# Moving masking from VectorE to ScalarE, with P*V a slot later, in a fused attention and FFN kernel

## The chip, the cores and the metric

One core of a Trainium2 chip runs the kernel. The metric is device time in microseconds (us) for one execution, lower is better. The profile and the trace are those of one execution. A run counts as "slow" when it took over 1.5% longer than the fastest run of the same kernel, else as "fast".

## The reference

Attention with a threshold, then a multiplicative FFN without a nonlinearity. There are 8 batches, 8 heads, 576 positions and 64 dimensions per head.

```python
scores = scale * np.matmul(q, k.transpose(0, 1, 3, 2))
thresh = np.max(scores, axis=-1, keepdims=True) - tau
scores = np.where(scores >= thresh, scores, -1000000000.0)
attn = np.exp(scores - max); attn = attn / (sum(attn) + 1e-09)    # shortened
x = attn @ v, heads side by side                                   # (4608, 512)
a = x @ w1; b = x @ w2
out = (a * b @ w3) @ w_out
```

## The kernel before

The kernel is a hand-made pipeline of slots. Heads go in 32 pairs, and a pair has nine chunks of 128 query rows by 576 keys: four for each head, and one *mixed* chunk that holds the last 64 rows of both heads. There are 288 chunks. P*V is the product of probabilities and values. PSUM is the memory that the kernel's matmuls write to; a piece of it can be used again once another engine has read it out. Slot `t` starts the scores of chunk `t` on TensorE, the maximum of chunk `t-1` on VectorE, and the masking of chunk `t-4`. Masking has two paths:

- Path P: ScalarE takes the exponential (0.67 us) one slot ahead, VectorE masks with one *select* (0.87 us).
- Path A: ScalarE does all of it in two passes, `mask_a` (0.77 us) in the chunk's slot and `mask_b` (0.67 us) one slot later.

The finished probabilities are transposed by DMA (for the first pairs by TensorE), and P*V of a whole pair starts a fixed number of slots after its last chunk. FFN matmuls fill TensorE's time in between.

```python
LAG = 4
EARLY = 4                      # pairs whose probabilities TensorE transposes
PATH = "AAP"                   # chunk c takes PATH[c % 3]; a mixed chunk is c = 9 n + 8
...
def mask_b(c):
    nc.scalar.activation(place(*stream[c]), chunks.pop(c)["y"][:, :], AF.Exp, scale=-CUT)
    leave_probs(*stream[c])                    # starts the transpose
...
def select(c):
    t = chunks.pop(c)
    nc.vector.scalar_tensor_tensor(out=place(*stream[c]), in0=t["sc"][:, :], scalar=t["thr"],
                                   in1=t["e"][:, :], op0=ALU.is_ge, op1=ALU.mult)
    leave_probs(*stream[c])
...
for units, follow in groups:                   # when P*V of a pair runs
    c = max(where[n, 8 if i == 4 else 2 * i + hh] for n, hh, i in units)
    c = max(c + LAG + 3, last + 2)
    at(c, attended, att, 0.9)                  # P*V, first half
    at(c + 1, attended, att, 0.9)              # P*V, second half
    norms[c + 2] = att                         # normalise on VectorE
    at(c + 3, attended, att, 0.35)             # transpose the result
...
for t in range(end + 1):                       # one slot
    scores(t)
    maximum(t - 1)
    if t in norms:
        next(norms[t])
    leave()                                    # what is left of the FFN steps
    while late:
        late.pop(0)()                          # PSUM copies of transposes
    ...
    c = t - LAG
    if PATH[c % 3] == "A":
        mask_a(c)
        waiting.append(c)
    while waiting and waiting[0] < c:
        mask_b(waiting.pop(0))
    if PATH[(c + 1) % 3] == "P":
        exponent(c + 1)
    if PATH[c % 3] == "P":
        select(c)
    ...
```

(The tests that a chunk number is in range are cut.)

With `9 n + 8` modulo 3 always 2, **every mixed chunk of the kernel before (the last batch aside) takes path P**. No line of the code says so; it follows from the period of three.

The softmax here doesn't subtract the row's maximum and nothing guards it: scores larger than these inputs give would overflow.

## Time and profile before

| | before |
|---|---|
| time, median of 4 runs | 565.11 us (563.97 to 567.57) |
| TensorE / VectorE / ScalarE busy | 488 / 453 / 389 us of 564.0 |
| 37th maximum pass starts at | 84.6 us |
| 253rd maximum pass starts at | 456.6 us |
| last maximum pass starts at | 514.8 us |

The maximum passes, one per chunk, are a good clock for the pipeline: the 37th ends the start-up, from the 37th to the 253rd the kernel is in its steady middle, after the last one only FFN work is left. Their times are read from the trace.

First, the page of the kernel before: busy time with its share of the span and the number of instructions, then the shares of the chain of waits.

```profile
PE 488.2 (87%) x4964; PEld 334.6 (59%) x4964; DVE 452.7 (80%) x1046; ACT 389.3 (69%) x678; POOL 182.2 (32%) x256
...
PE 43%; DVE 30%; DMA 10%; issue 7%; ACT 7%; POOL 2%; SPq 1%; DVEq 0%; ACTq 0%; POOLq 0%
```

The chain passes through both TensorE (PE) and VectorE (DVE). The table of windows tells where: from 100 to 450 us both are near 90% busy, and from 30 to 60 us VectorE is at 94%. Columns are the stretch, its length, busy us of each engine with the number of instructions, the granted TensorE clock, the DMA share and GB/s.

```profile
30.00:60.00 30.00, 22.40 (x262) 17.39 (x261) 28.32 (x58) 16.36 (x27) 23.73 (x35) 0.89 0.97 202
60.00:100.00 40.00, 33.40 (x409) 25.06 (x407) 32.72 (x76) 23.43 (x40) 10.60 (x12) 0.96 0.23 49
100.00:450.00 350.00, 319.21 (x3308) 218.60 (x3306) 312.53 (x723) 270.18 (x470) 127.05 (x161) 0.99 0.91 188
```

What TensorE waited for from 100 to 450 us (total us, times, longest):

```profile
PE S L244 <- DVE sc L269: 11.6, 12, 1.7
PE av L356 <- DMA pT<-pm: 6.6, 5, 2.7
PE S L250 <- DVE sc L269: 3.4, 5, 1.6
```

`S` are scores, waiting for the maximum pass to free their PSUM; `av` is P*V, waiting for transposed probabilities. The last FFN parts, in the timeline of TensorE (start, length, instruction):

```profile
547.25 0.60 PE L428 MATMUL ab<-xm,w1b 128*128 128x256 bf16 x4
548.00 0.60 PE L428 MATMUL ab<-xm,w2b 128*128 128x256 bf16 x4
548.43 0.60 PE L428 MATMUL ab<-xm,w1b 128*128 128x256 bf16 x4
```

From one step to the next (two groups of four) 1.18 us pass. A group that follows at once starts 0.43 us after the one before, so the work is 0.87 us, and 0.31 us of a step is lost. It is read as a wait for one of two PSUM banks; the list of waits does not name it, and part 5 of the change tests it.

Finally two groups of VectorE, with mean ns of one:

```profile
L335 DVE SCALAR_TENSOR_TENSOR pm<-sc,thr,e 128x576 bf16<-128x576 f32 x66 | 57.2, 866 | 11.4 <-ACT e L331 11.2
L277 DVE TENSOR_SCALAR thr<-mx 128x3 f32<-128x3 f32 x96 | 34.2, 356 | 0.0
```

The first waits 11 us for the exponential. The second, the subtraction that makes the threshold, has a median of 162 ns but a mean of 356: 28 of its 96 instances take 0.44 to 1.13 us (0.80 in the mean), and all 28 overlap a GpSimd operation.

### The profile page before, as it was taken

To read this page: it belongs to the slowest core of one execution; us is meant where nothing else is said; L and a number is where in the kernel's file an instruction comes from. 1 tells how busy PE (TensorE), PEld (TensorE's weight loads), DVE (VectorE), ACT (ScalarE), POOL (GpSimd) and SP (SyncE) were. 2 spreads that over 40 slices of the span, in tenths; PEclk is the share of its full clock that TensorE was granted. 3 is DMA by queue.
4 is the path that set the end of the run, shared out by engine and by line. 5 is a ranking of instruction groups with operands and counts; after the bars stand their busy time and mean duration, and the time that the engine had idled before them with its cause. 6 is when DMAs were issued, how large, how long until landed. Compare 5 with 4: busy or idle time off the path is not lost.

```text
span 564.0 us, 13012 instructions
## 1 busy us (share of the span) xinstructions
PE 488.2 (87%) x4964; PEld 334.6 (59%) x4964; DVE 452.7 (80%) x1046; ACT 389.3 (69%) x678; POOL 182.2 (32%) x256
## 2 busy tenths in 40 slices
PE   1777987988999889899899889999988899798985
PEld 0555665655666566565666567666656666465663
DVE  1899878989997998689899979899879977695321
ACT  2455555777887778668788778878867778588332
POOL 3986423063402632172305440353165300000000
PEclk9988989999999999999999999999989999799999
DMA  7997520987889697989999796989999667456310
GB/s 157 278 237 154 110 59 23 199 177 168 154 180 239 134 208 168 256 124 179 220 193 188 157 238 149 215 143 221 223 197 242 119 141 157 78 85 160 52 65 39
DMA packets 203374, 91.43 MB, mean 162 GB/s; under 512 B 169008, under 2 KB 194608, under 8 KB 203312
## 3 DMA queue, kind: packets, MB, share of 16 engines
q1 hardware_dynamic: 199920, 85.36, 71.1%
q0 software_dynamic: 3392, 5.24, 5.5%
q8 instruction: 39, 0.64, 0.5%
q14 instruction: 23, 0.19, 0.1%
HBM read 39.32 MB, written 9.44 MB: 86 GB/s over the span
## 4 chain that ended last, share of the span: by engine, by line
PE 43%; DVE 30%; DMA 10%; issue 7%; ACT 7%; POOL 2%; SPq 1%; DVEq 0%; ACTq 0%; POOLq 0%
PE ab L428 11%; DVE sc L269 11%; PE yp L443 10%; PE S L244 9%; PE av L356 4%; DVE ab L420 4%; DMA pT<-pm 4%; DVE pm L335 3%; DVE thr L277 3%; DMA pTm<-pms_74 3%; ACT y L321 2%; DVE pms_75 L335 2%; PE tp L205 2%; PE wp L132 2%; PE S L250 2%
## 5 line engine op out<-in xcount | busy, mean ns | idle before, releaser
L269 DVE TENSOR_SCALAR_CACHE_REDUCE sc<-S 128x576 f32<-128x576 f32 x288 | 213.4, 749 | 19.8 <-PE S L244 16.9
L321 ACT ACTIVATE y<-sc,thr 128x576 bf16<-128x576 f32 x192 | 140.6, 768 | 62.7 <-DVE thr L277 62.4
L244 PE MATMUL S<-kT,qT 128*128 128x288 bf16 x464 | 127.5, 294 | 15.1 <-DVE sc L269 11.8
L325 ACT ACTIVATE pm<-y 128x576 bf16<-128x576 bf16 x190 | 127.6, 672 | 1.5 <-DMA pT<-pm 1.4
L244 PE MATMUL S<-kB,qT 128*128 128x288 bf16 x464 | 127.3, 294 | 0.5 <-DMA kB<-kT 0.5
L244 PEld LDWEIGHTS <-qT 128*128 128x128 bf16 x928 | 89.0, 100 | 64.9 <-issue 17.0
L420 DVE TENSOR_TENSOR ab<-ah,ab 128x512 bf16<-128x512 bf16 (+1 forms) x88 | 51.7, 587 | 36.8 <-PE ab L428 32.2
L417 ACT ACTIVATE ah<-ab 128x512 bf16<-128x512 f32 (+1 forms) x88 | 45.2, 514 | 41.0 <-PE ab L428 39.4
L428 PE MATMUL ab<-xm,w2b 128*128 128x512 bf16 (+1 forms) x288 | 68.8, 362 | 4.1 <-DVE ab L420 0.9
L443 PE MATMUL yp<-wcb,ab 128*128 128x512 bf16 x288 | 71.2, 379 | 1.3 <-DVE ab L420 1.2
L428 PE MATMUL ab<-xm,w1b 128*128 128x512 bf16 (+1 forms) x288 | 68.0, 359 | 2.2 <-DVE ab L420 2.2
L335 DVE SCALAR_TENSOR_TENSOR pm<-sc,thr,e 128x576 bf16<-128x576 f32 x66 | 57.2, 866 | 11.4 <-ACT e L331 11.2
L331 ACT ACTIVATE e<-sc 128x576 f32<-128x576 f32 x96 | 64.3, 670 | 0.0
L356 PEld LDWEIGHTS <-pT 128*128 128x128 bf16 x1320 | 51.2, 98 | 11.8 <-DMA pT<-pm 7.6
L428 PEld LDWEIGHTS <-w2b 128*128 128x128 bf16 x352 | 33.3, 98 | 28.3 <-issue 10.2
L428 PEld LDWEIGHTS <-w1b 128*128 128x128 bf16 x352 | 33.0, 98 | 24.9 <-issue 6.3
L165 POOL CAST khl<-kf 128x512 bf16<-128x512 f32 x31 | 19.9, 641 | 72.9 <-PE tp L205 41.8
L166 POOL TENSOR_TENSOR qhl<-qf,qhl 128x512 bf16<-128x512 f32 x32 | 39.0, 1220 | 10.8 <-ACT qhl L568 8.3
L443 PEld LDWEIGHTS <-ab 128*128 128x128 bf16 x288 | 26.8, 98 | 24.8 <-issue 1.7
L166 POOL TENSOR_TENSOR khl<-kf,khl 128x512 bf16<-128x512 f32 x31 | 39.0, 1258 | 2.5
L435 ACT ACTIVATE ys<-yp 128x512 f32<-128x512 f32 x36 | 21.4, 595 | 25.0 <-PE yp L443 24.4
L165 POOL CAST khlt<-kt 128x256 bf16<-128x256 f32 x7 | 3.6, 511 | 95.5 <-DMA kt<-in_k_dram 95.5
(124 smaller groups left out, 778.6 us busy)
## 6 DMA issues: line engine op xcount, KB each, us to landing
kB<-kT SPq DMA_DIRECT2D x58, 144.0 KB, 4.0
out_dram<-ys SPq DMA_DIRECT2D x16, 512.0 KB, 3.6
kf<-in_k_dram SPq DMA_DIRECT2D x15, 512.0 KB, 4.5
qf<-in_q_dram SPq DMA_DIRECT2D x15, 512.0 KB, 5.6
vf<-in_v_dram SPq DMA_DIRECT2D x15, 512.0 KB, 4.8
pT<-pm SPq DMA_TRANSPOSE x112, 3.8
kt<-in_k_dram SPq DMA_DIRECT2D x16, 64.0 KB, 5.1
w1b<-in_moe_w_dram POOLq DMA_DIRECT2D x4, 256.0 KB, 6.0
```

Source lines behind the costliest of these rows:

```text
L166: lo.tensor_tensor(hl[1], src, hl[0], ALU.subtract)
L244: nc.tensor.matmul(sp[:, half, 0:HB], lhsT=t["qT"][:, q0:q0 + 128], rhs=kk[w][:, c0:c0 + HB], start=(w == 0), stop=(w == 1))
L269: nc.vector.tensor_scalar(sc[:, :].rearrange("p (a b) -> p a b", a=2), sp[:, :, 0:HB], 1.0, -3e38, ALU.mult, ALU.max, accum_out=maxima[c / ...
L321: nc.scalar.activation(t["y"][:, :], t.pop("sc")[:, :], AF.Prelu, scale=-1.0, bias=t.pop("thr"), alpha=0.125 / CUT)
L325: nc.scalar.activation(place(*stream[c]), chunks.pop(c)["y"][:, :], AF.Exp, scale=-CUT)
L331: nc.scalar.activation(t["e"][:, :], t["sc"][:, :], AF.Exp, scale=0.125)
L335: nc.vector.scalar_tensor_tensor(out=place(*stream[c]), in0=t["sc"][:, :], scalar=t["thr"], in1=t["e"][:, :], op0=ALU.is_ge, op1=ALU.mult)
L356: nc.tensor.matmul(dst, lhsT=lhsT, rhs=rhs, start=(g == 0), stop=(g == 4))
L417: return lambda: nc.scalar.activation(ah[:, 0:nt], p[:, 0:nt], AF.Copy)
L420: return lambda: nc.vector.tensor_tensor(ab[:, 0:nt], ah[:, 0:nt], p[:, 0:nt], ALU.mult)
L428: nc.tensor.matmul(p[:, 0:nt], lhsT=w[:, c, f * 128:(f + 1) * 128], rhs=x(c), start=(c == 0), stop=(c == 3))
L443: nc.tensor.matmul(yp[0:c1 - c0, :], lhsT=abs_[f][:, c0:c1], rhs=wcb[:, f, :], start=(f == 0), stop=(f == NF - 1))
```

## The change

Its intent is to take work off VectorE, and to give transposes and the last FFN parts more room.

1. `PATH` becomes `"AAAP"`: VectorE masks 72 chunks in place of 96. The exponential comes two slots ahead, with a third buffer.
2. The op on row sums of mixed chunks goes; 1e30 in the sums' column makes the reciprocal of the unwanted sums vanish.
3. P*V starts one slot later (not in the last batch); normalisation stands behind the select; the result's transpose comes a slot later; four buffers in place of two for mixed chunks.
4. Early transposes cover three pairs in place of four, and ScalarE makes part of the PSUM copies.
5. After the last slot, FFN steps use the three larger PSUM buffers of the scores.

```diff
-    EARLY = 4
+    EARLY = 3
+    LATER = 4
...
+            nc.gpsimd.memset(t[96:97, :, 0, D:D + 1], 1e30)
+            nc.gpsimd.memset(t[64:65, :, 1, D:D + 1], 1e30)
...
-    PATH = "AAP"
+    PATH = "AAAP"
...
+            if i % 2:
+                late.append(lambda: nc.scalar.activation(to, fro, AF.Copy))
+            else:
+                late.append(lambda: nc.vector.tensor_copy(to, fro))
...
-        if len(mixed) == 2:
-            nc.vector.tensor_tensor(rcp[:, 1, nu - 2:nu], rcp[:, 1, nu - 2:nu], diag[:, :], ALU.mult)
...
+                if w is w1b and wide():
+                    both = psum.tile([128, 2, 512], FP32, tag="S", name="both", bufs=3)
+                    p = both[:, 0, :]
...
-        c = max(c + LAG + 3, last + 2)
+        c = max(c + LAG + (LATER if units[0][0] < NPAIR - NP else 3), last + 2)
...
-        at(c + 3, attended, att, 0.35)
+        at(c + 4, attended, att, 0.35)
...
-            if t in norms:
-                next(norms[t])
             leave()
...
-            if 0 <= c + 1 < total and PATH[(c + 1) % 3] == "P":
-                exponent(c + 1)
-            if 0 <= c < total and PATH[c % 3] == "P":
+            if 0 <= c + 2 < total and PATH[(c + 2) % 4] == "P":
+                exponent(c + 2)
+            if 0 <= c < total and PATH[c % 4] == "P":
                 select(c)
+            if t in norms:
+                next(norms[t])
```

(Cut: the test for path "A", buffer counts, among them eight in place of ten for transposed probabilities, the removed constants, the FFN's start a slot later, the slot counter that `wide()` reads.)

More of the change, by code (lines that the diff above doesn't have):

```diff
@@ L59 @@
     ident2 = constp.tile([128, 64], BF16, tag="ident2", name="ident2")
-    diag = constp.tile([128, 2], FP32, tag="diag", name="diag")
     w1b = constp.tile([128, 4, d_ff], BF16, tag="w1b", name="w1b")
@@ L64 @@
     xt = constp.tile([128, NP, B, R], BF16, tag="xt", name="xt")
-    pms = [constp.tile([128, 640], BF16, tag=f"pms{i}", name=f"pms{i}") for i in range(2)]
+    pms = [constp.tile([128, 640], BF16, tag=f"pms{i}", name=f"pms{i}") for i in range(4)]
     vbs = [constp.tile([128, 2, 4, VW], BF16, tag=f"vb{i}", name=f"vb{i}") for i in range(5)]
@@ L72, in constants @@
     def constants():
-        nc.gpsimd.memset(diag[:, :], 0.0)
-        for hh in range(2):
-            nc.gpsimd.memset(diag[64 * hh:64 * hh + 64, hh:hh + 1], 1.0)
         nc.vector.tensor_tensor(ident2[:, :], ident[:, 0:64], ident[:, 64:128], ALU.add)
@@ L87, in constants @@
             nc.gpsimd.memset(t[:, S:640], 0.0)
+            nc.gpsimd.memset(t[0:64, S:S + 1], 1.0)
+            nc.gpsimd.memset(t[64:128, S + 32:S + 33], 1.0)
     wl = {}
@@ L284, in place @@
             pairs[n]["pm"] = work.tile([128, 2, S], BF16, tag="pm", name="pm", bufs=3)
-        return pairs[n]["pm"][:, hh, :] if hh < 2 else pms[n % 2][:, 0:S]
+        return pairs[n]["pm"][:, hh, :] if hh < 2 else pms[n % 4][:, 0:S]
     turning = []
@@ L291, in turn_probs @@
         nb = 9 if i < 4 else 5
-        pT = work.tile([128, nb, 128], BF16, tag="pT" if i < 4 else "pTm", name="pT", bufs=10 if i < 4 else 5)
+        pT = work.tile([128, nb, 128], BF16, tag="pT" if i < 4 else "pTm", name="pT", bufs=8 if i < 4 else 5)
         pairs[n]["pT", i] = pT
@@ L299, in go @@
             clock["pe"] += 0.07 * nb
-            late.append(lambda: nc.vector.tensor_copy(pT[:, :, :].rearrange("p g f -> p (g f)"), tp[:, 0:nb * 128]))
+            to, fro = pT[:, :, :].rearrange("p g f -> p (g f)"), tp[:, 0:nb * 128]
+            if i % 2:
+                late.append(lambda: nc.scalar.activation(to, fro, AF.Copy))
+            else:
+                late.append(lambda: nc.vector.tensor_copy(to, fro))
         turning.append(go)
@@ L309, in leave_probs @@
         elif hh == 1:
-            t["pT", i] = work.tile([128, 9, 128], BF16, tag="pT", name="pT", bufs=10)
+            t["pT", i] = work.tile([128, 9, 128], BF16, tag="pT", name="pT", bufs=8)
             nc.sync.dma_start_transpose(t["pT", i][:, :, :], t["pm"][:, :, :].rearrange("p a b -> p (a b)"))
         elif hh == 2 and n < EARLY:
-            turn_probs(n, 4, pms[n % 2][:, :])
+            turn_probs(n, 4, pms[n % 4][:, :])
         elif hh == 2:
             t["pT", 4] = work.tile([128, 5, 128], BF16, tag="pTm", name="pTm", bufs=5)
-            nc.sync.dma_start_transpose(t["pT", 4][:, :, :], pms[n % 2][:, :])
+            nc.sync.dma_start_transpose(t["pT", 4][:, :, :], pms[n % 4][:, :])
     def mask_a(c):
@@ L329, in exponent @@
         t = chunks[c]
-        t["e"] = work.tile([128, S], FP32, tag="e", name="e", bufs=2)
+        t["e"] = work.tile([128, S], FP32, tag="e", name="e", bufs=3)
         nc.scalar.activation(t["e"][:, :], t["sc"][:, :], AF.Exp, scale=0.125)
@@ L345, in attend @@
         nu = len(units) // 2
-        mixed = [j for j, (n, hh, i) in enumerate(units) if i == 4]
         for un, (n, hh, i) in enumerate(units):
@@ L360, in attend @@
         nc.vector.reciprocal(rcp[:, :, 0:nu], a5[:, :, :, D])
-        if len(mixed) == 2:
-            nc.vector.tensor_tensor(rcp[:, 1, nu - 2:nu], rcp[:, 1, nu - 2:nu], diag[:, :], ALU.mult)
-        elif mixed:
-            r = rcp[:, :, 0:nu].rearrange("p a (u h) -> p a u h", h=2)
-            nc.vector.tensor_tensor(r, r, diag[:, :].unsqueeze(1).unsqueeze(1).to_broadcast([128, 2, nu // 2, 2]),
-                                    ALU.mult)
         x = work.tile([128, 10, D], BF16, tag="x", name="x", bufs=2)
@@ L409, in leave, with wide @@
             pending.append(way)
+    def wide():
+        return clock["slot"] >= end
     def ffn(x, nt, store):
@@ L423, in ffn @@
             ah = work.tile([128, 512], BF16, tag="ah", name="ah", bufs=2)
-            ab = work.tile([128, 512], BF16, tag="ab", name="ab", bufs=12)
+            ab = work.tile([128, 512], BF16, tag="ab", name="ab", bufs=9)
+            both = None
             for w in (w1b, w2b):
-                p = psum.tile([128, 512], FP32, tag="m", name="ab")
+                if w is w1b and wide():
+                    both = psum.tile([128, 2, 512], FP32, tag="S", name="both", bufs=3)
+                    p = both[:, 0, :]
+                elif both:
+                    p = both[:, 1, :]
+                else:
+                    p = psum.tile([128, 512], FP32, tag="m", name="ab")
                 for c in range(4):
@@ L470 @@
     background = []
-    clock = {"pe": 0.0}
+    clock = {"pe": 0.0, "slot": 0}
     def step():
@@ L551 @@
         norms[c + 2] = att
-        at(c + 3, attended, att, 0.35)
+        at(c + 4, attended, att, 0.35)
         if follow:
-            at(c + 4, lambda follow: push(*[f(*a) for f, *a in follow]), follow)
-    end = last + 5
+            at(c + 5, lambda follow: push(*[f(*a) for f, *a in follow]), follow)
+    end = last + 6
     with tc.manual_schedule():
@@ L583 @@
         for t in range(end + 1):
+            clock["slot"] = t
             if t < total:
@@ L596 @@
             c = t - LAG
-            if 0 <= c < total and PATH[c % 3] == "A":
+            if 0 <= c < total and PATH[c % 4] == "A":
                 mask_a(c)
@@ L616 @@
                     step()
+        clock["slot"] = end
         while step():
```

## The prediction

> **What bounds the kernel now.** No engine is saturated over the span. TensorE is busy 488 of 564.0 us, VectorE 453, ScalarE 389 (the page's first part). From 100 to 450 us (table of windows) TensorE is busy 91%, VectorE 89%, ScalarE 77%: TensorE and VectorE hold each other up in turn. The chain of waits agrees: TensorE 43%, VectorE 30%, DMA 10%. TensorE is visibly idle 31 us in that middle: 12 us before scores, mostly on VectorE's maximum pass that frees their PSUM, 8 us before P*V, mostly on DMA transposes. From 30 to 100 us it is idle 14 us, 11 before the early probability transposes, again on VectorE. From 533 us on, each FFN step takes 1.18 us although its eight matmuls need 0.87 us: two PSUM banks do not let TensorE run ahead.
>
> **What changes, in durations of this trace.**
> - Masking by VectorE falls from 96 to 72 chunks: 24 x 0.80 us (866 ns less overlap) = 19 us off VectorE; ScalarE gets 24 x 0.77 = 18 us more.
> - The op on row sums goes: 29 x 0.19 = 5.6 us off VectorE.
> - Early transposes: 20 PSUM copies (14 us) on VectorE become 9 (6 us). Six move to ScalarE, an estimated 1.1 us each from its 0.59 us for 512 columns and 0.38 us for 256. The fourth pair's five go to DMA, little used then (23% from 60 to 100 us); TensorE loses 3 us.
> - Sum: VectorE -33 us, ScalarE +25 us (some 82% in the middle), TensorE -3 us.
> - P*V a slot later, four buffers for mixed chunks and an earlier exponential remove waits: 7 us of TensorE on transposes, 3 us of VectorE on one, part of 14 us in which VectorE waits for the exponential.
> - Last FFN parts: 16 steps lose 0.31 us each, 5 us, all critical.
> - Against it: normalisation now stands behind the select, so P*V's PSUM comes free about 1 us later, once per pair; DMA, 0.86 to 0.98 busy through most of the middle, gets more transposes and less time.
>
> Not touched: 28 of the 96 threshold subtractions take about 0.8 us instead of 0.16, and all 28 overlap a GpSimd operation. The Trainium skill, "SBUF — State Buffer", says that VectorE and GpSimd share a port pair held as an exclusive lock; these durations agree.
>
> **How much is critical.** Early stage: 5 us. Middle: VectorE loses about 18 us; I count half, 9 us, plus 3 us of removed DMA and exponential waits, less 2 us for the later norm: 10 us. Tail: 5 us. Sum 20 us: 544 us. TensorE then runs at about 94% in the middle.
>
> **Predicted: 544 us, 534 to 556 with 8 in 10. Faster by over 2%: 0.77; within 2%: 0.21; slower: 0.02.**
>
> **What would show the steps.** 72 selects, VectorE busy near 420, ScalarE near 413. Middle: TensorE's waits for the maximum pass fall from 12 to about 6 us, those for transposes to near 0. Early: the 11 us of idle before probability transposes fall under 5. Tail: FFN steps 0.87 us apart.
>
> **What would make it wrong.** ScalarE works in order and now carries two passes for three chunks running; if masks come late, transposes and P*V shift and VectorE's freed time turns into waits on ScalarE. DMA near saturation could make transposes later than the extra slot hides. The later norm could hold scores' PSUM. Then 555 or more. Or the coupling was tighter than half: 535.

## The result and the profile after

| | before | after |
|---|---|---|
| time, median of 4 runs each | 565.11 us | 546.32 us (545.83 to 547.55) |
| ratio | | 0.9665 (95% interval 0.9625 to 0.9706) |
| TensorE / VectorE / ScalarE busy | 488 / 453 / 389 us | 476 / 416 / 408 us |
| up to the 37th maximum pass | 84.6 us | 79.7 us |
| 37th to 253rd | 372.0 us | 365.0 us |
| 253rd to the last | 58.2 us | 54.1 us |
| after the last | 49.2 us | 45.7 us |

A ratio is the mean time of one kernel's fast runs over that of the other's in the same rounds, so it is not quite the quotient of the medians. Where two experiments are compared below, the quotient of their ratios to the kernel before is used, since not all ran on the same chip.

The total lies 2 us from the forecast. The page after:

```profile
PE 475.8 (87%) x4862; PEld 329.5 (61%) x4923; DVE 416.1 (76%) x982; ACT 407.5 (75%) x708; POOL 179.5 (33%) x267
...
PE 55%; DMA 13%; DVE 13%; ACT 10%; issue 6%; POOL 2%; SPq 0%; DVEq 0%; POOLq 0%; ACTq 0%
```

VectorE has left the chain (30% to 13%), as hoped, but DMA has grown in it. The same windows after:

```profile
30.00:60.00 30.00, 23.68 (x296) 17.45 (x296) 26.29 (x62) 24.40 (x38) 22.92 (x34) 1.00 1.01 220
60.00:100.00 40.00, 35.79 (x424) 26.01 (x429) 34.81 (x78) 31.69 (x55) 11.96 (x14) 1.00 0.59 118
100.00:450.00 350.00, 318.07 (x3281) 218.96 (x3322) 291.97 (x690) 280.12 (x490) 125.25 (x162) 0.98 0.93 188
```

In the middle VectorE fell from 313 to 292 us of 350, but TensorE is not busier than before (318 against 319 us). The waits of TensorE in the same stretch tell why:

```profile
PE av L361 <- DMA pTm<-pms_73: 11.7, 5, 2.6
PE ab L438 <- DVE ab L423: 3.3, 4, 1.1
PE av L361 <- DMA pTm<-pms_75: 2.7, 4, 1.3
PE tp L207 <- DVE thr L279: 2.5, 3, 1.9
PE av L361 <- DMA pT<-pm: 1.8, 2, 1.6
...
PE av L361 <- DMA pTm<-pms_76: 0.6, 1, 0.6
```

The waits of scores for the maximum pass are all but gone (0.2 us). In their place stand waits of P*V for `pTm`, the transposed **mixed** chunk. They total 15.0 us here, 14.4 of them on tiles that ScalarE wrote (`pms_76` is VectorE's); the prediction had waits for transposes at near 0. One such wait in the timeline after:

```profile
100.60 0.67 ACT L331 ACTIVATE pms_73<-y 128x576 bf16<-128x576 bf16 x1
101.68 1.56 SPq L317 DMA_TRANSPOSE pT<-pm  x1
103.35 0.52 SPq L149 DMA_DIRECT2D vf<-in_v_dram  x1
...
103.96 1.22 SPq L322 DMA_TRANSPOSE pTm<-pms_73  x1
...
110.46 0.30 PE L361 MATMUL av<-vb_81,pTm 128*128 128x65 bf16 x4 [2.61 <-DMA pTm<-pms_73]
```

The mixed chunk is finished by ScalarE (ACT) at 101.3 us. Its transpose is issued 2.7 us later, behind other DMA issues, lands at 110.4 us, and TensorE has stood still for 2.6 us. In the kernel before VectorE wrote this tile. Such a wait has a second price, which the granted clock (the third column from the right) shows around it:

```profile
107.00:110.40 3.40, 0.85 (x23) 0.69 (x17) 0.77 (x2) 3.29 (x6) 0.00 (x0) 1.00 1.37 160
110.40:114.00 3.60, 3.32 (x19) 1.94 (x21) 1.99 (x6) 0.00 (x0) 2.06 (x5) 0.53 1.21 228
```

After this stretch TensorE runs at half speed: the matmuls of scores start 0.24 us apart while the clock is low, 0.12 us otherwise (medians of the trace). The Trainium skill, "TensorE: Matmul & The Clock Gate", section "What's actually happening", describes this: the clock is gated by recent activity, to half after an idle window of about 3.4 us. This trace agrees on the half and on the length: each record of a low clock is at 0.5 and lasts 3.41 us or a multiple, apart from the last, which the end of the run cuts short. It does not agree that the window has to be idle: TensorE was still busy for 0.85 of the 3.4 us shown.

The tail after:

```profile
529.41 0.60 PE L438 MATMUL both<-xm,w1b 128*128 128x256 bf16 x4
529.85 0.60 PE L438 MATMUL both<-xm,w2b 128*128 128x256 bf16 x4
530.28 0.60 PE L438 MATMUL both<-xm,w1b 128*128 128x256 bf16 x4
```

Steps are now 0.87 us apart, as forecast.

### The profile page after: what moved, and what is told of

It is laid out like the page before. It is cut to its first block, busy times and chain, and to the rows that moved or that the text cites. A ratio compares the mean times of both kernels' runs of the same rounds, so it can differ in the third digit from the quotient of the medians.

```text
span 544.5 us, 12959 instructions
## 1 busy us (share of the span) xinstructions
PE 475.8 (87%) x4862; PEld 329.5 (61%) x4923; DVE 416.1 (76%) x982; ACT 407.5 (75%) x708; POOL 179.5 (33%) x267
## 4 chain that ended last, share of the span: by engine, by line
PE 55%; DMA 13%; DVE 13%; ACT 10%; issue 6%; POOL 2%; SPq 0%; DVEq 0%; POOLq 0%; ACTq 0%
PE ab L438 14%; PE S L246 13%; PE yp L453 10%; PE av L361 6%; DMA pTm<-pms_73 5%; DVE sc L271 4%; PE tp L207 4%; DMA pTm<-pms_75 4%; ACT y L327 3%; PE both L438 3%; DVE ab L423 2%; PE wp L134 2%; ACT pm L331 2%; DMA pT<-pm 2%; DVE pm L341 2%
## 5 line engine op out<-in xcount | busy, mean ns | idle before, releaser
L327 ACT ACTIVATE y<-sc,thr 128x576 bf16<-128x576 f32 x216 | 162.3, 769 | 20.4 <-DVE thr L279 20.4
L420 ACT ACTIVATE ah<-ab 128x512 bf16<-128x512 f32 (+1 forms) x72 | 39.5, 549 | 48.5 <-PE ab L438 46.8
L453 PE MATMUL yp<-wcb,ab 128*128 128x512 bf16 x268 | 68.5, 381 | 2.5 <-DVE ab L423 0.7
L423 DVE TENSOR_TENSOR ab<-ah,ab 128x512 bf16<-128x512 bf16 (+1 forms) x72 | 45.1, 626 | 27.5 <-PE ab L438 22.9
L438 PE MATMUL ab<-xm,w2b 128*128 128x512 bf16 x210 | 57.3, 389 | 5.2 <-DVE ab L423 3.3
L341 DVE SCALAR_TENSOR_TENSOR pm<-sc,thr,e 128x576 bf16<-128x576 f32 x64 | 58.7, 917 | 2.9 <-DMA pT<-pm 2.7
L438 PE MATMUL ab<-xm,w1b 128*128 128x512 bf16 x204 | 56.4, 379 | 3.0 <-ACT xm L391 1.0
L361 PEld LDWEIGHTS <-pT 128*128 128x128 bf16 x1310 | 47.6, 98 | 6.7 <-DMA pT<-pm 2.0
L337 ACT ACTIVATE e<-sc 128x576 f32<-128x576 f32 x72 | 48.5, 673 | 0.0
L168 POOL TENSOR_TENSOR qhl<-qf,qhl 128x512 bf16<-128x512 f32 x32 | 37.0, 1157 | 11.1 <-ACT qhl L578 8.5
```

The lines of the kernel that those rows point to most:

```text
L168: lo.tensor_tensor(hl[1], src, hl[0], ALU.subtract)
L327: nc.scalar.activation(t["y"][:, :], t.pop("sc")[:, :], AF.Prelu, scale=-1.0, bias=t.pop("thr"), alpha=0.125 / CUT)
L337: nc.scalar.activation(t["e"][:, :], t["sc"][:, :], AF.Exp, scale=0.125)
L361: nc.tensor.matmul(dst, lhsT=lhsT, rhs=rhs, start=(g == 0), stop=(g == 4))
L420: return lambda: nc.scalar.activation(ah[:, 0:nt], p[:, 0:nt], AF.Copy)
L423: return lambda: nc.vector.tensor_tensor(ab[:, 0:nt], ah[:, 0:nt], p[:, 0:nt], ALU.mult)
```

## The experiments

All were correct. Each had six timed runs beside 11 of the kernel before. Differences to the changed kernel are worked out from the ratios, on 546.3 us.

### Undo the masking share

```diff
-    PATH = "AAAP"        # and c % 4, (c + 2) % 4
+    PATH = "AAP"         # and c % 3, (c + 2) % 3
```

> The changed kernel with a third of the chunks masked by VectorE again (all else of the change kept; all mixed chunks are then VectorE's again). Theory 1, VectorE's relief of 19 us pays about half: 8 us slower than the changed kernel (554 us), VectorE busy near 435. Rival, the relief is eaten because the mixed chunks that moved to ScalarE are masked a slot later and their transposes then hold TensorE: at most 3 us slower (549 us or less), and TensorE's waits before P*V fall from 17 us in the middle to under 6.

Measured: 535.95 us (533.5 to 539.3), ratio 0.9481. That is 10 us **faster** than the changed kernel. Theory 1 falls; the rival's bound (549 us or less) holds, but it did not say that the time would fall. So the first headline of the change costs time. VectorE was busy 435 us, as expected. TensorE's waits in the middle:

```profile
PE tp L207 <- DVE thr L279: 5.8, 7, 1.9
PE S L252 <- DVE sc L271: 3.4, 7, 0.8
```

Waits for a mixed chunk's transpose are down to 0.4 us. The rival's mechanism fits; how far the time would fall it did not say.

### Undo the later slot of P*V

```diff
-    LATER = 4
+    LATER = 3
```

> The changed kernel with P*V at its old slot, all else kept. Theory, the later slot pays for mixed chunks that ScalarE masks a slot later: waits before P*V rise from 17 us to 40 or more in the middle, 10 to 20 us slower (557 to 566 us). Rival, the slot is not needed: waits rise by under 8 us and the time by under 3.

Measured: 584.31 us (580.54 to 585.89), ratio 1.0318: 37 us slower than the changed kernel, and slower than the kernel before. The mechanism was as expected, the size twice so. The window and the waits of TensorE, 100 to 450 us:

```profile
100.00:450.00 350.00, 299.96 (x2916) 201.02 (x2914) 255.84 (x604) 249.50 (x434) 104.58 (x141) 0.92 0.82 168
```

```profile
PE av L361 <- DMA pTm<-pms: 32.3, 14, 4.5
PE av L361 <- DMA pT<-pm: 13.7, 12, 3.1
```

46 us of waits for transposes fall in this stretch, 29 more than in the changed kernel. The granted clock is 0.92 in it: the trace records 58 of the 350 us at half speed, against 14. Half of the difference, 22 us, is an estimate of what that costs. Waits and clock together are more than the 37 us measured, for TensorE's other waits fell by some 9 us. So a wait costs more than its own length, which is the likely reason that the size was off.

### The same share, but VectorE keeps the mixed chunks

```diff
-            if 0 <= c < total and PATH[c % 4] == "P":
+            if 0 <= c < total and path(c) == "P":     # likewise for "A" and for c + 2
...
+    def path(c):
+        n, u = stream[c]
+        if n >= NPAIR - NP:
+            return PATH[c % 4]
+        return "P" if u in (3, 8) or (u == 5 and n % 4 == 0) else "A"
```

> The changed kernel with the same number of VectorE chunks (72), but so chosen that every mixed chunk before the last batch is among them. Theory, the new waits before P*V come from mixed chunks that ScalarE masks a slot later: these waits fall from 17 us to under 6 in the middle and the time by 5 to 8 us, to 538 to 541. Rival, they come from the input loads that share the DMA engines in those slots: waits above 12 us and the time within 2 us of 546.

Measured: 531.68 us (528.35 to 535.61), ratio 0.9396: 15 us faster than the changed kernel. The number of VectorE chunks is the same 72 and the input loads are the same; only which chunks they are differs.

```profile
PE av L367 <- DMA pT<-pm: 3.8, 5, 1.1
PE av L367 <- DMA pTm<-pms: 2.7, 3, 1.4
```

The waits for transposes in the middle fell from 16.8 to 6.5 us. The theory's direction holds; the rival as it was put falls, since the loads are the same and the waits went (what the loads may still add is told at the end of "Why the prediction was right or wrong"). The size was again more than the waits alone: the trace has 3.4 us at half clock in the middle in place of 13.7, by the same estimate 5 us, which with 10 us of waits make the 15. Against the run with a third of the chunks on VectorE (0.9481), a quarter is now 5 us faster (0.9%, the intervals of the two ratios do not overlap): that is what the relief of VectorE is worth when VectorE keeps the mixed chunks.

### A third on VectorE, but every mixed chunk on ScalarE

```diff
-    PATH = "AAAP"        # and c % 4, (c + 2) % 4
+    PATH = "PAA"         # and c % 3, (c + 2) % 3
```

> The changed kernel with a third of the chunks on VectorE (96, as before) but turned by one, so that every mixed chunk before the last batch is masked by ScalarE a slot later. Theory, it is who masks the mixed chunk that costs: waits of TensorE before P*V of 15 to 25 us in the middle and 545 to 552 us, although the share is that of the run at 536 us. Rival, the share itself costs (ScalarE's load): about 536 us and waits under 6 us.

Measured: 553.06 us (552.02 to 559.41), ratio 0.9816. With the same 96 VectorE chunks as the run at 536 us it is 3.5% or 19 us slower; only the turn of the pattern differs. The waits of TensorE in the middle:

```profile
PE av L361 <- DMA pTm<-pms: 11.5, 9, 2.3
PE S L246 <- DVE sc L271: 6.8, 7, 1.6
```

With 3.1 us on other transposes the waits are 14.6 us, just under what the theory expected, and the time 1 us above its range. Both pairs of runs say the same: who masks the mixed chunk weighs more (15 and 19 us) than whether VectorE masks a third or a quarter (5 us).

### The masking share alone, on the kernel before

```diff
-    PATH = "AAP"         # and c % 3, (c + 1) % 3
+    PATH = "AAAP"        # and c % 4, (c + 1) % 4
```

> The kernel before with a quarter of the chunks on VectorE and nothing else changed: three of four mixed chunks go to ScalarE, a slot later, with P*V at its old slot. Theory: 15 to 30 us slower than before (580 to 595 us), with waits before P*V of 35 us or more in the middle. Rival, the relief of 19 us of VectorE pays by itself as predicted: 3 to 9 us faster than before.

Measured: 595.78 us, the median of the five fast runs (592.61 to 597.76), ratio 1.0542: 5.4% slower than before. The profiled run is the slow one (605.44 us), so its waits, 34 us for transposes in the middle, are told with that caution. The relief alone is a loss.

### The later slot alone, on the kernel before

```diff
-        c = max(c + LAG + 3, last + 2)
+        c = max(c + LAG + (4 if units[0][0] < NPAIR - NP else 3), last + 2)
```

> The kernel before with P*V one slot later in all but the last batch, nothing else. Theory, the kernel before held TensorE on transposes that landed just in time, more than the 8 us of visible idle say: 8 to 14 us faster (551 to 557 us) with waits for transposes near 0. Rival, worth only the visible 7 us or less: 559 to 565 us.

Measured: 566.36 us (561.65 to 569.03), ratio 1.0026 (0.9978 to 1.0074): nothing. The theory fell. TensorE's waits for transposes did go from 6.9 to 1.4 us, but those of scores for the maximum pass rose from 15.0 to 22.1 us. VectorE's own waits in the middle name a candidate:

```profile
DVE pms L335 <- ACT e L331: 6.5, 10, 1.2
...
DVE pm L335 <- ACT e L331: 3.6, 5, 1.1
```

For 10 us it stood before selects whose exponential was not ready. It had done so for 10 us in the kernel before as well; a run below takes this wait away.

### Both share and slot undone

```diff
-    LATER = 4
-    PATH = "AAAP"
+    LATER = 3
+    PATH = "AAP"
```

> The changed kernel with both the masking share and the slot of P*V undone (a third on VectorE, old slot). Together with the two single undos (536 and 584 us) and the change (546 us) it makes a square. Theory, the slot is worth about 10 us where VectorE masks the mixed chunks and 38 us where ScalarE does: 543 to 549 us. If the two parts simply added up: 574 us.

Measured: 549.21 us (545.1 to 550.43), ratio 0.9715, within 0.3 us of the theory's range. TensorE waited for transposes of plain chunks more than for mixed ones:

```profile
PE av L361 <- DMA pT<-pm: 18.7, 10, 3.0
PE av L361 <- DMA pTm<-pms: 4.5, 7, 1.6
```

With the slot they are 1.4 us ("Undo the masking share"). The square, all else as in the changed kernel:

| | P*V at its old slot | a slot later |
|---|---|---|
| a third, mixed chunks on VectorE | 549.2 (0.9715) | 536.0 (0.9481) |
| a quarter, three of four mixed chunks on ScalarE | 584.3 (1.0318) | 546.3 (0.9665) |

The slot is worth 13 us with mixed chunks on VectorE and 37 us without. The two parts do not add up: most of what the later slot brings in the change repairs what the masking share broke.

### The later slot with an earlier exponential, on the kernel before

```diff
-            if 0 <= c + 1 < total and PATH[(c + 1) % 3] == "P":
-                exponent(c + 1)
+            if 0 <= c + 2 < total and PATH[(c + 2) % 3] == "P":
+                exponent(c + 2)          # three buffers; nine for the FFN's products; P*V later
```

> The kernel before with P*V a slot later and the exponential two chunks ahead of the select in place of one (three buffers for it, nine for the FFN's products); the masking share stays a third. P*V later alone gave nothing (566 us). Theory, VectorE then stood in the way, 10 us of it waiting for the exponential in the middle: these 10 us go under 2, and the time falls by 6 to 10 us, to 556 to 560. Rival, the exponential's wait is off the critical path: 564 to 567 us.

Measured: 554.44 us (553.45 to 555.04), ratio 0.9804: 2.2% or 12 us faster than the later slot alone, slightly more than expected. No wait for the exponential is left in VectorE's list. The square says the same of the slot: with the exponential early it is worth 13 us, where the exponential was late it was worth nothing. Whether the earlier exponential pays without the later slot was not run, so how the 12 us divide stays open.

### The same, with normalisation behind the select

```diff
-            if t in norms:
-                next(norms[t])
             leave()
...
                 select(c)
+            if t in norms:
+                next(norms[t])
...
-        at(c + 3, attended, att, 0.35)
+        at(c + 4, attended, att, 0.35)       # and what follows a slot later
```

> As the run with the exponential two chunks ahead, and the normalisation of P*V moved behind the select, as the change has it. Theory, VectorE also stood waiting for P*V of the same slot while other work was ready (5 to 9 us): 4 to 8 us faster than that run, 546 to 554 us, which with the last FFN parts (5 us), the early transposes and the op on row sums leads to the 536 us of the change without its masking share. Rival, as the prediction had it, the later norm costs 2 us.

Measured: 559.98 us (556.58 to 562.83), ratio 0.9886: 5 us slower than the run before it. The theory fell, and the prediction's fear of the later norm was right in direction. VectorE's waits for P*V did vanish (8.2 to 0.6 us), but TensorE got a new wait, put down to the operation that follows the norm in VectorE's order:

```profile
PE tp L205 <- DVE thr L277: 8.8, 14, 2.1
```

In all 14 cases this operation ends within 0.1 us of the norm's last one, so the wait may as well be for the norm, which sets free PSUM that `tp` takes in turn. This run holds two edits, the norm's place and the transpose a slot later, and doesn't part them.

### Undo the early transposes, and undo the last FFN parts

```diff
-    EARLY = 3
+    EARLY = 4            # and all PSUM copies on VectorE
```

> The changed kernel with the early probability transposes of four pairs, all copied by VectorE, as before. Theory, as predicted: 5 us slower, 551 us, all of it before the 36th maximum pass, which then starts at about 85 us in place of 80. Rival, ScalarE's copies cost as much as VectorE's: within 2 us.

Measured: 555.99 us (553.43 to 558.89), ratio 0.9838: 10 us slower than the changed kernel, twice the forecast. Only 2 us lie before the 37th maximum pass (81.6 against 79.7 us). The other 7 us arise up to the 253rd; waits for mixed chunks' transposes are 19.5 us in place of 15.0. The edit also moves FFN steps: the order of TensorE's instructions, as the two programs issue them, differs in places up to the 149th maximum pass and is the same from there on, and 6.4 of the 7 us lie before that pass. So the new order is a likely cause, but no run parts it from the rest.

```diff
     def wide():
-        return clock["slot"] >= end
+        return False
```

> The changed kernel with the last FFN parts back in the two small PSUM banks. Theory: 16 steps of 0.31 us come back, 5 us slower (551 us), all of it after the last maximum pass (45.7 us there become about 50.5). Rival, the tail is held by something else: no change.

Measured: 553.07 us (547.98 to 555.03), ratio 0.9762: 5.5 us slower, and 50.8 us after the last maximum pass in place of 45.7. As expected.

### A version that beats both

```diff
-    LATER = 4
+    LATER = 5            # on top of VectorE keeping the mixed chunks
```

> The best run so far (a quarter on VectorE with every mixed chunk among them, 532 us) with P*V yet another slot later. Theory, its 6.5 us of TensorE's waits for transposes in the middle go to about 1 and the time to 526 to 530 us. Rival, the eight buffers of transposed probabilities or the longer pipeline take it back: 531 us or more.

Measured: 526.52 us (524.48 to 528.92), ratio 0.9313: 6.9% faster than the kernel before and 3.6% faster than the changed one. TensorE's waits for transposes are at 1.2 us; what is left is VectorE again:

```profile
PE S L252 <- DVE x L373: 5.0, 13, 0.8
PE ab L444 <- ACT ah L426: 2.9, 3, 1.3
```

## Why the prediction was right or wrong

**The total was right: 544 forecast, 546.3 measured, in the range. The account behind it for the middle was not.** Sums of the right size came from terms of the wrong size and, in one case, the wrong sign; that they came within 2 us is luck.

- *Tail: right.* "16 steps lose 0.31 us each, 5 us, all critical." Undoing it cost 5.5 us, and the steps are 0.87 us apart as forecast; the stretch after the last maximum pass itself shortened by 3.5 us. It was the one term read from a stretch where a single engine sets the pace.
- *Work moved: nearly right.* VectorE went to 416 us (forecast near 420), ScalarE to 408 (near 413), selects to 72. Six ScalarE copies took 1.13 us each (estimate 1.1). A part of VectorE's fall was not foreseen: threshold subtractions longer than 0.4 us fell from 28 to 12, and the group from 34.2 to 22.9 us.
- *Early stage: right in the traces, uncertain in size.* The start shortened by 4.9 us (forecast 5); TensorE's waits before the early transposes fell from 12.1 to 6.0 us, not quite under 5. Undone alone, 2 us came back there and 7 elsewhere.
- *Middle: the failed step.* "VectorE loses about 18 us; I count half, 9 us." In the change the masking share has the opposite sign: it costs 10 us. Moving from a period of three to a period of four moves three of four mixed chunks to ScalarE, which finishes a chunk one slot later than VectorE does. A pair's mixed chunk is its last, so its transpose is the last thing P*V waits for. The two experiments with equal shares show it: 15 us between the two quarters, 19 us between the two thirds. The relief by itself is worth 5 us, about half of the 9.
- *"3 us of removed DMA and exponential waits"*: mis-sized. With all else of the change in place the later slot is worth 13 us if VectorE keeps the mixed chunks, 37 us if it doesn't; on the kernel before it is worth nothing, and 12 us come when the exponential is made early with it. The 7 us of waits seen in the trace before were no bound: with the rest of the change and the old slot, 23 us of waits for transposes appear. That TensorE and VectorE hid each other's delays in the kernel before fits this, but is not shown by itself.
- *"Those for transposes to near 0"*: wrong, 16.8 us of them in the middle, and TensorE at 91% rather than 94%. The prediction did name the danger ("if masks come late, transposes and P*V shift"), but took it for a matter of ScalarE's load. It was above all a matter of which chunks the pattern hits.
- *"2 us for the later norm"*: the direction holds. 5 us were measured, together with the later result transpose and on another base, and the new wait of 8.8 us is of the kind that the prediction feared.

Why did the middle still gain 7 us? By the square, -13 us for the slot and +10 us for the share come on top of a rest that gains by itself: with share and slot undone the kernel is still 2.9% faster than before, and its middle 3.6 us shorter. Of this rest the FFN parts and the early transposes are measured. The op on row sums and the four buffers of mixed chunks were not run alone, so their part stays open, and so do the 4.1 us gained between the 253rd and the last maximum pass.

The later mask is not the whole cause of a wait. Of the mixed chunks that ScalarE masks in the changed kernel, only those of pairs with an even number are waited for (buffers 73 and 75, not 74). From pair 4 to pair 22 their transposes took 4.6 to 6.5 us from issue to landing, those of buffer 74 2.4 to 3.8 us. With every mixed chunk on ScalarE ("PAA") all nine waits again fall on even pairs. Input loads are issued in the slots of the even pairs, and the 107 to 110 us window shows the DMA engines crowded (the packets that start in it take 1.37 times the stretch). So with the later slot it takes a late mask and a slow transpose together. That the loads make the transpose slow is read from the trace, not tested; keeping the chunks on VectorE was enough without touching the loads.

## What to carry to other kernels

When a pipeline deals work out by a counter, look up which items each residue hits before counting engine time: a change of period can move the one item that the next stage waits for to the slower path. A term worked out as "half of the freed time" is a guess; ask first which event ends last in that stretch, and what the change does to that event. And judge parts of a compound change in pairs, since a part may only repair what another one broke.

## What the Trainium skill lacked or had wrong

- "TensorE: Matmul & The Clock Gate" tells of half clock after an idle window of about 3.4 us, and of oscillation. It does not say how busy a window may be and still count as idle. Here the clock fell to 0.5 after windows that were far from idle: before the four low records in the middle of the changed kernel TensorE was busy for 0.78 to 1.80 of the 3.41 us, before the eleven in the middle of the run with P*V at its old slot for 0.49 to 1.64. With waits of at most 4.5 us, the run with P*V at its old slot had a mean granted clock of 0.949 over its span against 0.992 for the run with a third on VectorE and the later slot, which has 1.4 us of such waits in the middle.
- "SBUF — State Buffer", section "SBUF: two separate sides", says that VectorE and GpSimd can block each other through a shared port pair. The traces agree: all 28 threshold subtractions longer than 0.4 us before (0.80 us in the mean, against a median of 0.16) and all 12 after overlap a GpSimd operation. But so do 22 of the 84 shorter ones after, so an overlap alone does not make one long. The page doesn't say how often two instruction streams will collide: the change doesn't touch GpSimd's work in the middle, yet the group's busy time fell from 34.2 to 22.9 us. The new order of VectorE's work within a slot is a likely cause, but no run tested it.
- "DMA: Bandwidth & Descriptors" gives a bandwidth of DMA transposes, but no time from the issue of a transpose to its landing under load. Here the transpose of one 128x640 tile took 2.4, 3.0 and 6.5 us (least, median, most); TensorE waited where it was long and the mask late.
